# An adaLN attention and MLP block on one core: GpSimd's memsets after the first norm, modulation weights in halves of rows, one row tile's statistics on ScalarE, and the MLP transposes on TensorE

## The chip, the cores and the metric

The kernel runs on one core of a Trainium2 chip. The metric is the device time of one execution in microseconds; the time of a kernel is the median of several runs. The engines are TensorE (PE; its weight loads are listed as PEld), VectorE (DVE), ScalarE (ACT), GpSimd (POOL) and SyncE (SP), which issues nearly all DMAs here.

## The reference, cut to what matters

2048 tokens of width 512, 32 heads of 16, an MLP of width 1376, bf16 in and out.

```python
def _A_ref(x, wqkv, wo):                       # H = 32 heads, Dh = 16
    q, k, v = split((x @ wqkv))                # 2048 x 512 each
    p = softmax(einsum('bhqd,bhkd->bhqk', q, k) * Dh ** (-0.5))
    return merge(einsum('bhqk,bhkd->bhqd', p, v)) @ wo

def _B_ref(x, w1, b1, w2, b2):
    return gelu(x @ w1 + b1) @ w2 + b2         # tanh form of gelu

mod = (silu(c) @ w_mod).reshape(1, 6, 1, 512)  # w_mod is 512 x 3072
sa, ca, ga, sb, cb, gb = mod[:, 0], ..., mod[:, 5]
h = layernorm(x) * (1 + ca) + sa
x = x + ga * _A_ref(h, A_wqkv, A_wo)
h = layernorm(x) * (1 + cb) + sb
x = x + gb * _B_ref(h, B_w1, B_b1, B_w2, B_b2)
```

The softmax is over all 2048 keys for each head and query, so 32 x 2048 x 2048 exponentials are needed. Attention does not depend on the order of the tokens as long as queries, keys, values and outputs use the same one.

## The kernel before

**Tiling.** The tokens are four blocks of 512 (`QB`), each of four row tiles of 128 (`TPB`). The widths are handled in four chunks of 128 columns. Attention is cut into 32 runs: for blocks 0 to 2 a run is one block of queries and four heads, for the last block it is half a block of queries and eight heads. Each run goes over 16 key tiles of 128 keys; a key tile of a run is four pieces of 128x512 scores. TensorE makes scores (line 850), an engine makes exponentials, and TensorE multiplies them with the values (line 1042) into one accumulator `od`, where a column of ones in the values (`VEB`) makes the denominators.

**Two ways of making exponentials.** ScalarE takes two or three pieces at a time from the score tiles `st` with its Exp function (line 900, written to `pt`). VectorE takes pieces from the small PSUM tiles `ax` (line 948): it adds a constant to scaled scores and writes int16, whose bits are a bf16 of about the exponential; four shifted copies (lines 980 and 1001, a part of the last on GpSimd, line 986) are multiplied with the values as well, which evens out the error. Which key tiles VectorE may take is fixed per run (`DKS`, four of 16; one in the first run); ScalarE takes over those that VectorE has not begun when its own are used up.

**What sets the order.** The order of instructions on each engine is made when the kernel is built. `Plan` is a small model of the engines: every piece of work is an `Op` with an engine, an estimated duration, dependencies, a priority, sometimes a resource to acquire and a gate (a function that says whether it may be chosen yet). `Plan.step` picks the next one, and its instructions are written out at that moment. Dependencies of an `Op` set only when the planner lets it start; what waits on the chip follows from the tiles that instructions write and read, and from dependencies added by hand (`behind`, `after_dve`). Priorities get a pseudo-random part from the list `SEEDS`, one number for each 12.5 us of planned time. When TensorE would be idle, the planner adds matmuls on zeros (`heat`, lines 443, 448, 459).

**The front.** `c` goes through silu and one small transpose into `sc` (line 580, ScalarE). SyncE loads the first block of tokens in two halves (line 506), then two blocks of 512 columns of `w_mod` (`load_mod`, line 513), then the first columns of the projection weights (line 526), which are held by hand until the first of the two `w_mod` loads has landed (`behind`). `mod_half` (line 604) multiplies `sc` with one `w_mod` block into four columns each, the shift (line 609) and one plus the scale (line 611), into `modA`.

`layer_norm` (line 647) does the norm of one block: statistics of each row tile on VectorE (`stats`, lines 619 and 620), the reciprocal roots for two row tiles at a time on GpSimd (`rstd`, lines 624 and 626), the normalised rows `z` on VectorE (`apply`, line 630), the transpose, and the modulation (`modulate`, line 635 on ScalarE, line 638 on VectorE). For the norms ahead of attention, TensorE transposes `z` into PSUM (lines 669 and 690). For the MLP's, which have no pair of PSUM resources (the last branch), a DMA transposes each row tile from `z` into `h` (line 706), and the modulation works in place on `h` (line 712). `z`, `h`, `st`, `ax` and `modA` carry the names under which they appear in the profile; `h` is there as `blk`. Two `ax` tiles serve VectorE's scores and all projections.

GpSimd zeroes the query tiles `qm` (line 751) and sets up the value tiles `VEB` (line 561); for all but the first block a gate (`first_ln`) lets the planner choose these only after the first norm's `z` are placed.

**The tail of a block.** `block_tail` (line 1239) runs the output projection, the residual, the second norm and the MLP of a finished block between the attention work of later ones; the first half of the last block has the same function with two row tiles, the second half is `last_half` (line 1315).

Of the kernel before, what the change touches and what calls it, by code (L numbers as in the profile page):

```python
# [56 lines left out]
SEEDS = (0, 21, 549, 0, 302, 149, 169, 905, 398, 171, 86, 267, 11, 0, 921, 757, 414, 415, 365, 131, 15, 618, 871, 673, 0, 7, 415, 859, 670, 71, 663, 730, 487, 227, 515, 667, 435, 149, 398, 986, 54, 601, 378, 422, 797, 441, 478, 923, 570, 539, 723, 939, 122, 117, 263, 722, 826, 101, 751, 0, 366, 0, 0, 0, 0, 0)  # L57
# [196 lines left out]
def kernel(  # L254
# [211 lines left out]
    x_src = A_x[0].rearrange("(b t p) d -> b p t d", t=TPB, p=P)  # L466
# [136 lines left out]

    def mod_half(i):
        w = o_wm[i]
        mm = chain([(lambda ps, m=m: mod_mm(ps, 0, w.tile, m, False), 0.22, 0.17 * (m % 2) + 0.01)
                    for m in range(NC)], [o_sc, o_warm, w], "modA", r_ax, [w])
        if i == 0:
            return op("DVE", lambda o: nc.vector.tensor_copy(out=modA[:, 0:NC], in_=mm.tile[:, 0:NC]), 0.2, (mm,),
                      prio=0.0, rel=(mm,))  # L610
        return op("DVE", lambda o: nc.vector.tensor_scalar(out=modA[:, NC:2 * NC], in0=mm.tile[:, 0:NC], scalar1=1.0,
                                                           scalar2=None, op0=ALU.add), 0.2, (mm,), prio=0.0, rel=(mm,))
    o_mA = op("NIL", None, 0.0, [mod_half(i) for i in range(2)], lat=0.0, prio=0.0)


    def stats(ln, t, src):
# [3 lines left out]
        nc.vector.bn_aggr(out=mv[:, t, :], in_=st6)  # L620

# [25 lines left out]
    def layer_norm(src, deps, mod, mod_dep, hold_z, alloc_h, engines, ps_res, kind, prio,  # L647
                   after=None, nt=TPB, by_part=False):
# [908 lines left out]
```

## Time and profile before

| What | Value |
| --- | --- |
| runs | 778.5, 780.29, 780.5 us; median 780.29 |
| profiled execution, its time | 777.76 us |
| its span, first to last instruction | 776.0 us |
| granted TensorE clock, mean over the span | 0.997 |
| ScalarE busy outside the exponentials | 749.1 - 707.3 = 41.8 us |
| first exponential starts | 16.20 us |
| last group of exponentials ends | 751.7 us |
| DMA engines' mean busy share, 0 to 20 us | 0.71 |

Times are microseconds, unless a column is said to be nanoseconds. A line of a group gives the source line, engine, operation, output and input tiles, shapes, the count, then the busy time and the mean duration in nanoseconds of one, then how long the engine stood idle ahead of these instructions and what ended most of that. A line of a timeline gives start and duration, then the same names, and in brackets the idle time before it and what released it. A line of the windows gives the stretch, its length, the busy time of PE, PEld, DVE, ACT and POOL, the granted clock, the DMA share and GB/s.

### The profile page before, as it was taken

The page shows a single profiled execution, that of the slowest core. Times are in us where ns is not written, and L with a number is a line of the kernel's source. Part 1 is how long each engine was busy: PE and PEld are TensorE (multiplying, and loading weights), DVE is VectorE, ACT ScalarE, POOL GpSimd, SP SyncE. Part 2 cuts the span into 40 slices and gives each one's busy share as a digit, 9 for nine tenths or more (in the row PEclk, how much of TensorE's full clock was granted, in tenths as well). Part 3 has the DMA queues.
Part 4 walks back from the last instruction along what each step waited for, and adds up shares of the span by engine and source line. Part 5 has one row for each costly group of instructions (what it writes and reads, how often), then busy time and mean ns, then how long its engine had stood idle before and what let it go on. Part 6 is the DMA issues. An engine that isn't in the chain of part 4 may idle for free. (4 is left out here: it accounts for less than half of the span.)

```text
span 776.0 us, 20631 instructions
## 1 busy us (share of the span) xinstructions
PE 720.0 (93%) x8218; PEld 271.0 (35%) x8288; DVE 717.8 (93%) x1196; ACT 749.1 (97%) x683; POOL 279.3 (36%) x615
## 2 busy tenths in 40 slices
PE   8899989999999899999989999999999999999997
PEld 3433423323333222323222233323234344344444
DVE  6868899899999999999999999999989998999974
ACT  3999999999999999999999999999999999999993
POOL 6222433444443334344444333332232332233330
PEclk9999999999999999999999999999999999999999
DMA  7007011000011101110101200001111021000200
GB/s 217 29 17 215 18 25 43 20 17 16 19 45 27 47 20 50 32 21 22 44 20 35 44 18 24 19 21 32 33 44 31 26 40 46 17 19 25 64 20 28
DMA packets 46690, 30.07 MB, mean 39 GB/s; under 512 B 25573, under 2 KB 41990, under 8 KB 46594
## 3 DMA queue, kind: packets, MB, share of 16 engines
q1 hardware_dynamic: 46586, 28.75, 13.6%
q8 instruction: 65, 1.06, 0.6%
q14 instruction: 31, 0.25, 0.1%
q10 hardware_dynamic: 8, 0.00, 0.0%
HBM read 21.30 MB, written 2.61 MB: 31 GB/s over the span
## 5 line engine op out<-in xcount | busy, mean ns | idle before, releaser
L900 ACT ACTIVATE pt<-st 128x1536 bf16<-128x1536 f32 x624 | 707.3, 1419 | 2.2 <-PE ax L850 1.2
L948 DVE TENSOR_SCALAR ph<-ax 128x512 int16<-128x512 f32 x488 | 320.3, 682 | 22.3 <-PE ax L850 20.1
L986 POOL TENSOR_TENSOR sl<-ph,step 128x128 int32<-128x128 int32 x352 | 162.3, 463 | 316.2 <-DVE ph L1001 85.2
L850 PE MATMUL st<-qm,kT 32*128 32x512 bf16 x1560 | 243.8, 382 | 32.6 <-ACT pt L900 25.4
L850 PEld LDWEIGHTS <-kT 32*128 32x128 bf16 x2048 | 85.7, 91 | 244.0 <-issue 234.5
L850 PE MATMUL ax<-qm,kT 32*128 32x512 bf16 x488 | 159.8, 379 | 5.5 <-DVE ph L948 2.7
L1042 PEld LDWEIGHTS <-VEB 128*32 128x32 bf16 x5024 | 110.5, 95 | 154.0 <-issue 129.2
L1001 DVE TENSOR_SCALAR sh<-ph 128x4096 int16<-128x4096 int16 x122 | 148.3, 1217 | 0.1
L1042 PE MATMUL od<-pt,VEB 128*32 128x512 bf16 (+1 forms) x1944 | 148.1, 342 | 0.2 <-DVE OD L1067 0.2
L1042 PE MATMUL od<-ph,VEB 128*32 128x512 bf16 (+1 forms) x1232 | 90.8, 338 | 2.0 <-DVE ph L1001 0.7
L1042 PE MATMUL od<-sh,VEB 128*32 128x512 bf16 (+1 forms) x1232 | 87.8, 338 | 0.3
L1001 DVE TENSOR_SCALAR ph<-ph 128x2048 int16<-128x2048 int16 x122 | 83.3, 685 | 0.4
L980 DVE TENSOR_SCALAR sl<-ph 128x1024 int16<-128x1024 int16 (+3 forms) x122 | 59.2, 488 | 0.3
L1094 POOL TENSOR_TENSOR OT<-OD,RB 128x128 bf16<-128x128 f32 x76 | 34.5, 458 | 55.8 <-DVE sh L1001 28.3
L1042 PE MATMUL od<-sl,VEB 128*32 128x512 bf16 (+1 forms) x616 | 49.1, 338 | 0.4 <-POOL sl L986 0.2
L1265 PE MATMUL ax<-blk,W 128*128 128x512 bf16 (+1 forms) x156 | 41.1, 352 | 1.3 <-issue 0.5
L1094 POOL TENSOR_TENSOR OS<-OD,RB 128x128 bf16<-128x128 f32 x48 | 22.9, 479 | 41.2 <-DVE sh L1001 24.1
L729 PE MATMUL ax<-blk,w 128*128 128x512 bf16 x96 | 31.0, 386 | 1.0 <-issue 0.5
L1269 DVE TENSOR_SCALAR g<-ax,b1c 128x512 bf16<-128x512 f32 x33 | 24.4, 743 | 1.2 <-PE ax L1265 1.1
L1209 PE MATMUL ax<-w,g 128*128 128x512 bf16 x85 | 24.8, 382 | 0.7 <-DVE ph L948 0.3
L619 DVE BATCH_NORM_STATS2 ln_s<-xb 128x6 f32<-128x512 bf16 x32 | 21.7, 677 | 2.6 <-DMA xb<-in_A_x_dram 2.5
L1067 DVE COPY OD<-od 128x512 f32<-128x512 f32 x31 | 21.1, 682 | 0.0
(121 smaller groups left out, 398.7 us busy)
## 6 DMA issues: line engine op xcount, KB each, us to landing
RB<-rn SPq DMA_DIRECT2D x124, 64.0 KB
xb<-in_A_x_dram SPq DMA_DIRECT2D x8, 512.0 KB
out_dram<-o SPq DMA_DIRECT2D x16, 128.0 KB
qm<-qs SPq DMA_DIRECT2D x120, 16.0 KB
W<-in_B_w_dram SPq DMA_DIRECT2D x1, 1376.0 KB
w<-in_A_wqkv_dram SPq DMA_DIRECT2D x3, 384.0 KB
blk<-in_w_mod_dram SPq DMA_DIRECT2D x2, 512.0 KB
g<-in_w_mod_dram SPq DMA_DIRECT2D x2, 512.0 KB
```

The lines of the kernel that those rows point to most:

```text
L729: return chain([(lambda ps, j=j, n=n: nc.tensor.matmul(out=ps[:, 0:QB], lhsT=w.tile[:, j, cc * P:(cc + 1) * P], rhs=o_h[b].tile[:, j, :], ...
L850: nc.tensor.matmul(out=o.tile[:, k * QB:(k + 1) * QB], lhsT=kT[cc][kb][rows, ko * P:(ko + 1) * P], rhs=qm.tile[rows, par, :] if hb is None ...
L900: nc.scalar.activation(out=e.tile[:, 0:len(got) * QB], in_=o.tile[:, 0:len(got) * QB], func=ACT.Exp, scale=ESC)
L948: nc.vector.tensor_scalar(out=ph.tile[:, c0:c0 + QB], in0=o.tile, scalar1=PH_B, scalar2=0.0, op0=ALU.add, op1=ALU.max)
L980: parts = [in_turn(op("DVE", lambda o: nc.vector.tensor_scalar(out=into.tile[:, 0:cols], in0=first.tile[:, 0:cols], scalar1=PH_SH[-1], sca ...
L986: after_dve(nc.gpsimd.tensor_tensor(out=into.tile[:, c].bitcast(I32), in0=first.tile[:, c].bitcast(I32), in1=step, op=ALU.add))
L1001: o = op("DVE", lambda o: nc.vector.tensor_scalar(out=dst(o), in0=src(), scalar1=PH_SH[j], scalar2=None, op0=ALU.add), us, deps, lat=DL, p ...
L1042: nc.tensor.matmul(out=o_od[r].tile[32 * i:32 * i + 32, n * HB:n * HB + w], lhsT=v_tile(kt)[:, c0:c0 + 32], rhs=got[i][:, at:at + w], star ...
L1094: two = beside(lambda c: nc.gpsimd.tensor_tensor(out=OT.tile[:, c], in0=OD.tile[:, c], in1=o5.tile[:, c], op=ALU.mult), (OT,), (OD, o5))
L1209: nc.tensor.matmul(out=ps, lhsT=g[:, f, col:col + P], rhs=rhs, start=(f == 0), stop=(f == NF - 1))
L1265: mm = chain([(lambda ps, f=f, j=j: nc.tensor.matmul(out=ps[:, 0:N], lhsT=W1[:, j, f * P:(f + 1) * P], rhs=h.tile[:, j, 0:N], start=(j == ...
L1269: ev.append(op("DVE", lambda o, f=f, mm=mm: nc.vector.tensor_scalar(out=g.tile[:, f, 0:N], in0=mm.tile[:, 0:N], scalar1=b1c[:, f:f + 1], s ...
```

## The change

Five things change, and the planner's seeds with them.

- The planner's memsets of `qm` and `VEB` (all but the first block's) depend on the first norm's last `z`, where they had a gate.
- The two first loads of `w_mod` take 256 rows and 1024 columns each, where they took 512 rows and 512 columns; the products of the first half of the rows go to `modP`, and the second half's are added to them.
- Row tile t of a block holds tokens 4p + t on partition p, where it held tokens 128t + p; outputs are stored accordingly.
- The statistics of the first block's fourth row tile are made by ScalarE, in two passes with a running sum.
- The MLP's norms are transposed by TensorE into `ax`, from where the modulation reads them; there were DMA transposes, with the modulation in place in SBUF.

```diff
-SEEDS = (0, 21, 549, 0, 302, 149, 169, 905, 398, 171, 86, ...)
+SEEDS = (629, 934, 166, 131, 246, 833, 618, 433, 157, 123, ...)
...
-    x_src = A_x[0].rearrange("(b t p) d -> b p t d", t=TPB, p=P)
+    x_src = A_x[0].rearrange("(b p t) d -> b p t d", t=TPB, p=P)
+    out_dst = out[0].rearrange("(b p t) d -> b p t d", t=TPB, p=P)
...
     def load_mod(i):
         def go(o):
-            first[i] = nc.sync.dma_start(out=o.tile, in_=wm_src[:, :, i * D:(i + 1) * D])
+            first[i] = nc.sync.dma_start(out=o.tile.rearrange("p (j h) n -> p j (h n)", h=2),
+                                         in_=wm_src[:, 2 * i:2 * i + 2, 0:2 * D])
...
-    def v_init(v, prio, gate):
+    def v_init(v, prio, after):
         x = v[..., 0:32 * VW].rearrange("p t (h w) -> p t h w", w=VW)
-        return [op("POOL", lambda o, to=to, c=c: nc.gpsimd.memset(to, c), 0.35, prio=prio, gate=gate)
+        return [op("POOL", lambda o, to=to, c=c: nc.gpsimd.memset(to, c), 0.35, after, prio=prio)
...
-    first_ln = [False]
-    for b in range(NQ):
-        late = (lambda: True) if b == 0 else (lambda: first_ln[0])
-        o_v0[b] = v_init(VEB[b], 1.0 + b, late)
+    o_v0[0] = v_init(VEB[0], 1.0, ())
...
     def mod_half(i):
         w = o_wm[i]
-        mm = chain([(lambda ps, m=m: mod_mm(ps, 0, w.tile, m, False), 0.22, 0.17 * (m % 2) + 0.01)
-                    for m in range(NC)], [o_sc, o_warm, w], "modA", r_ax, [w])
+        def go(ps, m):
+            for j in range(2):
+                nc.tensor.matmul(out=ps[:, m:m + 1], lhsT=w.tile.rearrange("p (j h) n -> p j (h n)", h=2)[
+                    :, j, m * P:(m + 1) * P], rhs=sc[:, 2 * i + j:2 * i + j + 1], start=(j == 0), stop=(j == 1))
+        mm = chain([(lambda ps, m=m: go(ps, m), 0.08, 0.17 * (m % 2) / 2 + 0.005) for m in range(2 * NC)],
+                   [o_sc, o_warm, w], "modA", r_ax, [w])
         if i == 0:
-            return op("DVE", lambda o: nc.vector.tensor_copy(out=modA[:, 0:NC], in_=mm.tile[:, 0:NC]), 0.2, (mm,),
-                      prio=0.0, rel=(mm,))
-        return op("DVE", lambda o: nc.vector.tensor_scalar(out=modA[:, NC:2 * NC], in0=mm.tile[:, 0:NC], scalar1=1.0,
-                                                           scalar2=None, op0=ALU.add), 0.2, (mm,), prio=0.0, rel=(mm,))
+            one = op("DVE", lambda o: nc.vector.tensor_copy(out=modP[:, 0:NC], in_=mm.tile[:, 0:NC]), 0.12, (mm,),
+                     prio=0.0, rel=(mm,))
+            two = op("DVE", lambda o: nc.vector.tensor_scalar(out=modP[:, NC:2 * NC], in0=mm.tile[:, NC:2 * NC], scalar1=1.0,
+                                                              scalar2=None, op0=ALU.add), 0.12, (mm,), prio=0.0, rel=(mm,))
+            return op("NIL", None, 0.0, (one, two), lat=0.0, prio=0.0)
+        return op("DVE", lambda o: nc.vector.tensor_tensor(out=modA, in0=mm.tile[:, 0:2 * NC], in1=modP, op=ALU.add),
+                  0.2, (mm, parts[0]), prio=0.0, rel=(mm,))
...
+    def stats_act(ln, t, src):
+        mv, _ = ln.tile
+        root = math.sqrt(D)
+        junk = work.tile([P, D], BF16, name="ln_j", bufs=1)
+        neg = work.tile([P, 1], FP32, name="ln_n", bufs=1)
+        nc.scalar.activation(out=junk, in_=src, func=ACT.Identity, scale=-1.0 / (D * root), accum_out=neg)
+        nc.scalar.activation(out=junk, in_=src, func=ACT.Square, bias=neg, scale=1.0 / root,
+                             accum_out=mv[:, t, 1:2])
+        nc.scalar.mul(mv[:, t, 0:1], neg, -root)
...
-        st = [op("DVE", lambda o, t=t: stats(ln, t, src(t)), 0.83, (deps[t], ln, after and after[t]), prio=prio)
+        st = [op("ACT", lambda o, t=t: stats_act(ln, t, src(t)), 1.7, (deps[t], ln), prio=prio) if t in on_act else
+              op("DVE", lambda o, t=t: stats(ln, t, src(t)), 0.83, (deps[t], ln, after and after[t]), prio=prio)
...
-            turned = [dma(lambda o, t=t: nc.sync.dma_start(
-                out=h.tile[:, :, t * P:(t + 1) * P], in_=z.tile[:, t, :], transpose=True),
-                (za[t], h), kb=P, n=2.8, prio=0.6, rel=(z,)) for t in range(nt)]
             for j in range(NC):
+                def tr(o, j=j):
+                    o.ps = o.tile.bitcast(BF16)[:, 0:nt * P]
+                    for t in range(nt):
+                        nc.tensor.transpose(out=o.ps[:, t * P:(t + 1) * P],
+                                            in_=z.tile[:, t, j * P:(j + 1) * P], identity=ident)
+                one = op("PE", tr, nt * 0.0705, za, lat=PEL, mode=("full", 0), kind=kind,
+                         acq=r_ax, rel=(z,))
+                trs.append(one)
                 e = engines[j]
-                done.append(op(e, lambda o, j=j, e=e: modulate(
-                    e, h.tile[:, j, 0:nt * P], h.tile[:, j, 0:nt * P], mod, j), 0.07 + nt * 0.068, turned + [mod_dep, h],
-                    prio=0.1, port=True))
+                done.append(op(e, lambda o, j=j, one=one, e=e: modulate(
+                    e, h.tile[:, j, 0:nt * P], one.ps, mod, j), 0.13 + nt * 0.1, (one, mod_dep, h), prio=0.1,
+                    rel=(one,)))
...
-    o_qz = [op("POOL", lambda o, n=n, p=p: nc.gpsimd.memset(QM[n][:, p, :], 0.0), 0.5, prio=0.5 + n, gate=lambda: first_ln[0])
-            for n in range(1, 4) for p in range(2)]
+    o_qz = []
...
-                out=out[0][b * QB + t * P:b * QB + (t + 1) * P, :], in_=a.tile), (a,), kb=128,
+                out=out_dst[b][:, t, :], in_=a.tile), (a,), kb=128,
...
-            ("DVE", "ACT") if b in PARTS else ("DVE", "DVE", "ACT", "ACT") if b < 3 else ("DVE",) * 4, tuple(r_st[::-1]) if b == 0 else (r_ax, r_ax), kind, 0.6 + 0.2 * b, after, by_part=b in PARTS)
+            ("DVE", "ACT") if b in PARTS else ("DVE", "DVE", "ACT", "ACT") if b < 3 else ("DVE",) * 4, tuple(r_st[::-1]) if b == 0 else (r_ax, r_ax), kind, 0.6 + 0.2 * b, after, by_part=b in PARTS,
+            on_act=() if b else (3,))
...
         if b == 0:
-            op("NIL", lambda o: first_ln.__setitem__(0, True), 0.0, za, lat=0.0, prio=0.0)
+            o_qz.extend(op("POOL", lambda o, n=n, p=p: nc.gpsimd.memset(QM[n][:, p, :], 0.0), 0.5, za[-1:], prio=0.5 + n)
+                        for n in range(1, 4) for p in range(2))
+            for nv in range(1, NQ):
+                o_v0[nv] = v_init(VEB[nv], 1.0 + nv, za[-1:])
```

More of the change, by code (lines that the diff above doesn't have):

```diff
@@ L602, in mod_columns @@
         return op("DVE", out_, 0.4, (mm,), prio=0.65, rel=(mm,))
+    modP = const.tile([P, 2 * NC], FP32, name="modP")
     def mod_half(i):
         w = o_wm[i]
[L606 to L613 removed]
+        def go(ps, m):
[4 more added lines that the diff above has]
+                   [o_sc, o_warm, w], "modA", r_ax, [w])
+        if i == 0:
+            one = op("DVE", lambda o: nc.vector.tensor_copy(out=modP[:, 0:NC], in_=mm.tile[:, 0:NC]), 0.12, (mm,),
[5 more added lines that the diff above has]
+                  0.2, (mm, parts[0]), prio=0.0, rel=(mm,))
+    parts = []
+    for i in range(2):
+        parts.append(mod_half(i))
+    o_mA = parts[1]
     def stats(ln, t, src):
@@ L1412, in last_half @@
             dma(lambda o, t=t, a=a: nc.sync.dma_start(
-                out=out[0][b * QB + t * P:b * QB + (t + 1) * P, :], in_=a.tile), (a,), kb=128,
+                out=out_dst[b][:, t, :], in_=a.tile), (a,), kb=128,
                 rel=(a,))
```

4 lines of the change are left out of this document (2 added, 2 removed).

## The prediction

> **What bounds the kernel now.** I read the page first (engine shares, costliest groups), then busy time by windows, then the timeline of the first 17 us, then single shapes. From the page:
>
> ```profile
> span 776.0 us, 20631 instructions
> PE 720.0 (93%) x8218; PEld 271.0 (35%) x8288; DVE 717.8 (93%) x1196; ACT 749.1 (97%) x683; POOL 279.3 (36%) x615
> ...
> L900 ACT ACTIVATE pt<-st 128x1536 bf16<-128x1536 f32 x624 | 707.3, 1419 | 2.2 <-PE ax L850 1.2
> L948 DVE TENSOR_SCALAR ph<-ax 128x512 int16<-128x512 f32 x488 | 320.3, 682 | 22.3 <-PE ax L850 20.1
> ...
> L1001 DVE TENSOR_SCALAR sh<-ph 128x4096 int16<-128x4096 int16 x122 | 148.3, 1217 | 0.1
> ...
> L1001 DVE TENSOR_SCALAR ph<-ph 128x2048 int16<-128x2048 int16 x122 | 83.3, 685 | 0.4
> L980 DVE TENSOR_SCALAR sl<-ph 128x1024 int16<-128x1024 int16 (+3 forms) x122 | 59.2, 488 | 0.3
> ```
>
> ScalarE's exponentials (L900) take 707 us and wait 2.2 us in all. A key tile is four 128x512 pieces of one run; there are 32 runs of 16 tiles, 512 in all. VectorE took 122 of them (L948 has 488 = 4 x 122), ScalarE the other 390. A tile costs ScalarE 4 x 707.3/1560 = 1.81 us, and VectorE (320.3 + 148.3 + 83.3 + 59.2)/122 = 5.01 us. Busy time by windows of 100 us (PE, PEld, DVE, ACT, POOL, clock, DMA):
>
> ```profile
> 200.00:300.00 100.00, 94.16 (x1018) 32.49 (x1021) 98.13 (x154) 100.00 (x90) 39.11 (x87) 1.00 0.13 34
> 600.00:700.00 100.00, 94.98 (x1473) 41.62 (x1481) 95.45 (x159) 99.94 (x86) 33.49 (x73) 1.00 0.12 31
> ```
>
> ScalarE has no gap in the long middle and VectorE almost none. So the time is three terms: the front until the first exponential (16.2 us), ScalarE's unbroken work (to 751.7 us), and a tail of 24.3 us. The middle gets shorter only if tiles move to VectorE. If VectorE gets x us more of other work, the two share it: x/5.01 / (1/1.81 + 1/5.01) = 0.27x us on the end. The front, from its timeline (start, duration, engine):
>
> ```profile
> 6.76 0.70 DVE L630 TENSOR_SCALAR z<-xb,mv,rs 128x512 bf16<-128x512 bf16 x2
> 6.93 0.29 POOL L624 TENSOR_SCALAR rs<-mv 128x2 f32<-128x2 f32 x1 [0.56 <-DVE mv L620]
> 7.30 0.74 POOL L626 TENSOR_TENSOR rs<-rs,mhalf 128x2 f32<-128x2 f32 x1
> 7.99 0.99 POOL L751 MEMSET qm<- 128x512 bf16 x2
> 8.36 0.16 DVE L609 COPY modA<-ax 128x4 f32<-128x4 f32 x1 [0.90 <-PE ax L586]
> 8.44 2.12 DVE L630 TENSOR_SCALAR z<-xb,mv,rs 128x512 bf16<-128x512 bf16 x2
> 10.62 0.93 PE L690 MATMUL st<-ident,z 128*128 128x128 bf16 x7 [0.78 <-DVE modA L611]
> 11.16 0.99 DVE L638 TENSOR_SCALAR blk<-st,modA 128x512 bf16<-128x512 bf16 x2 [0.53 <-PE st L690]
> 12.21 0.62 PE L729 MATMUL st<-blk,w 128*128 128x512 bf16 x1 [0.23 <-DVE blk L638]
> 16.20 6.88 ACT L900 ACTIVATE pt<-st 128x1536 bf16<-128x1536 f32 x6 [0.64 <-PE st L850]
> ```
>
> Statistics, rs, the four z, transposes, modulation, projections, scores, exponential: one chain. The second pair of z takes 2.12 us beside GpSimd's memsets, the first pair 0.70 without them. The clock (the last three columns are granted clock, DMA share, GB/s):
>
> ```profile
> 10.00:11.00 1.00, 0.38 (x4) 0.39 (x5) 0.63 (x2) 0.00 (x0) 1.00 (x3) 0.74 0.82 172
> 12.00:13.00 1.00, 0.79 (x2) 0.29 (x2) 0.15 (x1) 1.00 (x2) 1.00 (x4) 0.50 1.11 350
> 14.00:15.00 1.00, 1.00 (x10) 0.53 (x9) 0.58 (x3) 0.03 (x1) 0.00 (x0) 1.00 0.96 300
> ```
>
> From about 10.3 to 13.7 us TensorE ran at half clock, just where transposes and projections stand.
>
> **The change, part by part.**
>
> *Statistics of the fourth row tile on ScalarE.* VectorE loses one BATCH_NORM pair (0.66 + 0.18 us, 0.80 from start to start) and finishes the third at 6.05 instead of the fourth at 6.84. ScalarE does two passes of 128x512; the nearest row is its modulation, 1.45 us for two, plus 0.17 for a small ACTIVATE: 1.6 us, and what the running sum costs is not in the trace: between nothing and two more small ones (0.34). I take 1.8. The row tile is there between 4 and 5.17 us (VectorE took its neighbour at 5.17 without a wait); taking 4.5, ScalarE ends at 6.3, idle there anyway (3.59 us idle before L580). GpSimd's rs, at 6.93 before, starts at about 6.5 and ends at 7.6, not 8.04. `sc` (6.51) stands behind these passes on ScalarE; if they ended at 7, it and the modulation matmuls would be late by 0.5 us; these have that cover only while the weights land at 7.74.
>
> *Modulation weights in halves of rows, tokens by partition.* Bytes are the same; rows get 2 KB instead of 1 KB. The two modulation loads flow from about 4 to 9.1 us, 1 MB in 5.1 us, against 300 to 350 GB/s in the windows at 12 to 15 us, which would be 3.0 to 3.5. So between 0 and 2 us can go; I take 0.4 for the first load (7.74 to 7.3), nearer to nothing, since the engines were already busy with it most of the time (DMA share 0.91 and 0.90 in 5 to 7 us). One more small VectorE copy, 0.15. The column matmuls stay at 32. Projection weights wait for the first load and move with it. Out stores keep 1 KB rows, scattered by 4 KB: 0, off the path but for the last store.
>
> *The second pair of z.* It starts at 8.44 because L609 stands ahead of it in VectorE's queue and waits for the weights. If that order stays: 8.2. If the earlier rs puts z first: 7.6. I take z first, -0.84, since rs is now planned earlier than the weights; the other end is -0.2.
>
> *Memsets depend on the first norm.* The dependency is one of the planner's: it sets when a memset is planned, and issues no semaphore (where the code wants a real one it adds it by hand, as in `after_dve`). On GpSimd nothing stands between the second rs and the memsets before or after. I take 0; the bounds are 0 and -1.4 (2.12 - 0.70). In a sentence by itself: the Trainium skill's page "SBUF — State Buffer", section on the shared port pair, says that a VectorE operation of the two-port kind and a GpSimd one exclude each other; the 2.12 us agree, and if the change really kept the memsets out, the sum would be 1.4 us lower.
>
> *Clock.* Four of the eight projection matmuls start 0.42 us apart, not 0.21 (0.8 us), and the seven transposes took 0.93 where eight took 0.61 at full clock (0.4): 1.2 us. Before the drop TensorE stood idle 0.78 us for z; with z 0.84 earlier this gap goes. I take the whole 1.2; the ends are 0 and, if the drop moves onto the projections entirely, +0.8. The Trainium skill ("TensorE: Matmul & The Clock Gate", Part 1) says the window is free-running, about 3.4 us; the trace's stretch is that long, and by this rule the phase differs from run to run, so half the gain, 0.6, would be the mean, and the sum below 0.6 higher.
>
> *Front: -0.84 - 1.2 = -2.0 us* (from -3.4, with the memsets, to +1.0).
>
> *MLP transposes on TensorE.* 14 DMA transposes go (4 in each of three blocks, 2 in the last), with 1.2 us each of SyncE's queue and the 28 us that the queue stood at L706. TensorE on the critical side waited 1.0 us in all for the q rows of that queue: gain 0 to 1.0, taken 0. Added: 16 transposes a block and 8 in the last, 56; eight take 0.62, so 4.3 us of TensorE, hidden behind its fillers (L443 and L459: 20 us of records that are planned only where TensorE is free); without that cover it would be late for scores and cost 4.3. The modulation now reads PSUM:
>
> ```profile
> L638 DVE TENSOR_SCALAR blk<-blk,modB 128x512 bf16<-128x512 bf16 x12 | 4.3, 402 | 0.0
> L638 DVE TENSOR_SCALAR blk<-blk,modB 128x256 bf16<-128x256 bf16 x4 | 1.1, 344 | 0.0
> L638 DVE TENSOR_SCALAR blk<-ax,modA 128x256 bf16<-128x256 bf16 x8 | 2.7, 406 | 0.1
> L638 DVE TENSOR_SCALAR blk<-ax,modA 128x512 bf16<-128x512 bf16 x4 | 2.0, 540 | 1.3 <-PE ax L690 1.3
> ```
>
> 12 x 0.138 + 4 x 0.062 = 1.9 us of VectorE, so 0.27 x 1.9 = +0.5. Each of the 16 also takes one of two `ax` tiles from VectorE's scores: between nothing and one mean wait of L948 (20.1/38 = 0.53 us); I take nothing here.
>
> *New seeds.* The order is drawn anew. VectorE can take at most 125 tiles (4 a run, 1 in the first), 3 more, each 1.33 us by the shared rate and 1.81 at most: -5.4 at best, as much the other way for three fewer; the tail's order can shift by some 1.5. Taken 0.
>
> *Sum:* -2.0 + 0.5 = -1.5. The profiled execution took 777.76 us (span 776.0 and 1.76 around it), so 776.3; the median of the runs is 780.29, 2.5 above it, so **778.8**.
>
> **The rivals.**
>
> *VectorE becomes the bound (slower).* Place: the two `ax` tiles in the MLP blocks. If each of the 16 new takings costs L948 its 0.53 us, 8.5 + 1.9 = 10.4 us of VectorE, two whole tiles go back to ScalarE: 3.6 us; with 1.2 saved in the front and one tile more lost to the new order (1.3), 780.3 + 3.6 - 1.2 + 1.3 = 784. It decides from 2.3/0.27 = 8.5 us of VectorE upwards if the front gives nothing. For it: VectorE is 95 to 99% busy and PE ax is its main wait. Against: `ax` is already taken for some 50 q, k and v projections, and L1269 (33 evictions from `ax`) waited 1.2 us in all.
>
> *More goes to VectorE (faster).* SyncE's queue is free of 45 us of issue and standing, the front is about -2.9, and two of the three tiles move: 780.3 - 2.9 + 0.5 - 2.7 = 775. For it: VectorE still idles 20 us between 100 and 740 us. Against: those gaps are waits for TensorE, which gets more to do.
>
> *It doesn't do what it says.* Memsets run beside z as before, weights land as before, z stays behind the copy; the front gives 0 to 0.5, and +0.5 in the middle cancels it: 780.3.
>
> **How the numbers follow.** What a measurement of this kernel can tell is about 0.3%, 2.3 us. Forecast 0.48, its own range 776.5 to 781 (front -3.4 to 0, middle 0 to +1), of which 0.2 lies below 778.0. VectorE gains 0.18. VectorE bound 0.27. Nothing happens 0.07. Faster 0.2 + 0.18 = 0.38, and 0.02 more from the forecast with a better tail: 0.40; slower 0.27 and 0.02 from a worse tail: 0.29; the rest, 0.31, within. The range reaches from 773 (two tiles and the whole front) to 785 (the slower rival and a tail 1 us worse).
>
> **What would show it.** First L900 at about 14.2 us; rs for the third and fourth tiles at 6.5; z pair still about 2.1 us long beside L751; granted clock 1.00 in 10 to 14 us; L948 about 488 +- 4; L638 from `ax` at 0.54 us; L948's wait for PE ax near 20 us. It is wrong if L948 drops below 480, if ScalarE shows gaps in the middle, or if the first exponential isn't earlier.

## The result, and the profile after

The changed kernel takes 780.97 us (median of 20 runs, 778.18 to 785.15), the kernel before 778.40 us (20 runs, 776.91 to 781.29). The ratio is 1.0032, with a 95% interval of 1.0016 to 1.0048: it became slower by 2.5 us. The median of three runs that the prediction started from, 780.29, was 1.9 us above that of 20. Of all the runs of the experiments, one (821.81 us, the profiled run of the query rows one after the other) was in a slower state of the chip, and medians and ratios leave it out.

From here on, line numbers are those of the kernel that a line comes from; L927 of the changed kernel is L900 of the one before, L975 is L948, and L877 is L850. First the page of the changed kernel, to be laid beside the first lines of the prediction:

```profile
span 779.1 us, 20699 instructions
PE 732.7 (94%) x8299; PEld 276.2 (35%) x8299; DVE 713.5 (92%) x1188; ACT 752.8 (97%) x690; POOL 283.2 (36%) x632
...
L927 ACT ACTIVATE pt<-st 128x1536 bf16<-128x1536 f32 x626 | 708.9, 1408 | 5.1 <-PE st L877 3.2
L975 DVE TENSOR_SCALAR ph<-ax 128x512 int16<-128x512 f32 x484 | 317.6, 683 | 27.1 <-PE ax L877 24.6
```

L975 has 484 pieces, not 488: VectorE got 121 tiles, one fewer, and it waits longer for TensorE (24.6 us against 20.1) though it has less to do. ScalarE's exponentials now wait 5.1 us, not 2.2. Windows of the changed kernel (PE, PEld, DVE, ACT, POOL, clock, DMA share, GB/s):

```profile
500.00:600.00 100.00, 96.16 (x1095) 33.79 (x1097) 95.16 (x149) 98.36 (x84) 30.92 (x68) 0.98 0.10 28
600.00:700.00 100.00, 94.14 (x1470) 42.05 (x1462) 94.33 (x157) 98.02 (x84) 34.34 (x77) 1.00 0.10 28
```

In the last one ScalarE was busy 99.94 us before and is busy 98.02 now. Its timeline (start, length of an unbroken group, and in brackets the wait ahead of it) shows where; first the changed kernel, then the kernel before:

```profile
563.03 11.47 ACT L927 ACTIVATE pt<-st 128x1536 bf16<-128x1536 f32 x10 [1.33 <-PE ax L877]
...
606.15 78.32 ACT L927 ACTIVATE pt<-st 128x1536 bf16<-128x1536 f32 x69 [1.92 <-PE st L877]
...
755.93 1.28 ACT L1301 ACT_TABLE_LOAD   x1
```

```profile
573.38 5.99 ACT L900 ACTIVATE pt<-st 128x1536 bf16<-128x1536 f32 x5 [0.25 <-PE st L850]
580.31 88.25 ACT L900 ACTIVATE pt<-st 128x1024 bf16<-128x1024 f32 x78 [0.94 <-PE ax L850]
...
751.70 1.28 ACT L1274 ACT_TABLE_LOAD   x1
```

The table load ends the exponentials: 755.93 against 751.70. With the first exponential at 15.97 against 16.20 us, the two profiled executions differ like this:

| Term | Before | After | Difference |
| --- | --- | --- | --- |
| front, to the first exponential | 16.20 | 15.97 | -0.23 |
| middle, to the last table load | 735.50 | 739.96 | +4.46 |
| tail, to the end of the span | 24.30 | 23.17 | -1.13 |
| span | 776.0 | 779.1 | +3.1 |

Of the 4.46, one tile more on ScalarE is 1.81. The listed waits of its exponentials between 20 and 752 us sum to 3.67 (0.17, 1.33, 0.25, 1.92) against 1.47 (0.28, 0.25, 0.94), which is 2.20 more. By the windows from the first exponential to the last table load, ScalarE was busy 735.85 us against 733.73, 2.12 more, and idle 2.34 more: the tile is most of the first, the listed waits are most of the second.

The granted clock explains part of the spread of the runs: among those with a mean clock of 0.999 or more, the changed kernel's median is 778.65 (5 of 20 runs), that of the kernel before 777.51 (13 of 31 runs beside the first experiments), which leaves 1.1 of the 2.5 us. The mean over all of these runs is 0.9966 for the changed kernel and 0.9976 for the kernel before.

The front of the changed kernel:

```profile
5.66 1.06 PE L443 MATMUL ax<-warm 128*128 128x512 bf16 x2
...
7.89 0.17 PE L576 MATMUL ax<-ident,sr 4*128 4x4 bf16 x1
...
9.62 0.54 PE L610 MATMUL ax<-sc,blk 128*128 128x1 bf16 x16 [0.15 <-PE ax L443]
```

```profile
6.26 0.74 DVE L652 TENSOR_SCALAR z<-xb,mv,rs 128x512 bf16<-128x512 bf16 x2 [0.36 <-POOL rs L648]
10.20 0.16 DVE L617 TENSOR_SCALAR modP<-ax 128x4 f32<-128x4 f32 x1 [3.20 <-PE ax L610]
10.27 0.15 DVE L615 COPY modP<-ax 128x4 f32<-128x4 f32 x1
10.34 0.85 DVE L652 TENSOR_SCALAR z<-xb,mv,rs 128x512 bf16<-128x512 bf16 x2
```

```profile
8.10 0.17 ACT L579 ACTIVATE sc<-ax 128x4 bf16<-128x4 bf16 x1 [2.04 <-PE ax L576]
```

The first modulation matmul (L610) needs its weights and `sc`, which ScalarE had at 8.27 us. SyncE has one wait for these weights, 4.2 us long; it issues two loads of projection columns ahead of it (2.64 and 3.15 us) and the next at 8.05, when the wait is over. So the weights landed at about 8.05 us, not earlier than in the kernel before (7.74), and L610 stood ready from 8.27 to 9.62 us, 1.35 us, behind fillers (L443, L448) on TensorE's queue. In the kernel before, its counterpart was released by the weights:

```profile
7.77 0.46 PEld L586 LDWEIGHTS <-blk 128*128 128x128 bf16 x16 [0.60 <-DMA blk<-in_w_mod_dram]
```

The second pair of z stood behind the two copies of the columns on VectorE, which waited 3.20 us for L610.

This front is one draw. Five of the experiments below leave its instructions as they are (without the MLP transposes, more fillers, one tile fewer, and both on the query rows), and their profiles have the first exponential at 15.22, 15.69, 15.08, 16.03 and 15.88 us. In all six, L610 starts 1.72 or 1.73 us behind the small transpose of L576, with the same fillers between the two. What moves is L576, from 6.87 to 7.89 us: the fillers ahead of it start 0.43 us apart at first and 0.22 apart later, and the step from one to the other lies anywhere between 4.8 and 6.9 us. The clock column reads 1.00 on both sides of it, so this step is read from the spacing alone.

### The profile page after: what moved, and what is told of

The parts are those of the page before. It is cut to its first block, busy times and chain, and to the rows that moved or that the text cites. A ratio compares the mean times of both kernels' runs of the same rounds, so it can differ in the third digit from the quotient of the medians.

```text
span 779.1 us, 20699 instructions
## 1 busy us (share of the span) xinstructions
PE 732.7 (94%) x8299; PEld 276.2 (35%) x8299; DVE 713.5 (92%) x1188; ACT 752.8 (97%) x690; POOL 283.2 (36%) x632
## 4 chain that ended last, share of the span: by engine, by line
ACT 52%; PE 31%; issue 9%; DVE 7%; SPq 1%; DMA 0%; POOL 0%; DVEq 0%; ACTq 0%; POOLq 0%
ACT pt L927 50%; PE od L1069 10%; PE st L877 9%; DVE ph L975 3%; PE ax L1292 2%; PE ax L1236 2%; PE ax L877 2%; PE ax L757 2%; PE t L1236 1%; DVE sh L1028 1%; PE ax L443 1%; PE ax L1230 1%; DVE ph L1028 1%; PE t L1421 1%; ACT g L1307 1%
## 5 line engine op out<-in xcount | busy, mean ns | idle before, releaser
L927 ACT ACTIVATE pt<-st 128x1536 bf16<-128x1536 f32 x626 | 708.9, 1408 | 5.1 <-PE st L877 3.2
L975 DVE TENSOR_SCALAR ph<-ax 128x512 int16<-128x512 f32 x484 | 317.6, 683 | 27.1 <-PE ax L877 24.6
L1013 POOL TENSOR_TENSOR sl<-ph,step 128x128 int32<-128x128 int32 x369 | 168.9, 459 | 315.3 <-DVE sh L1028 103.0
L877 PE MATMUL st<-qm,kT 32*128 32x512 bf16 x1564 | 245.0, 382 | 29.1 <-ACT pt L927 22.3
L877 PEld LDWEIGHTS <-kT 32*128 32x128 bf16 x2048 | 88.2, 91 | 247.3 <-issue 233.6
L877 PE MATMUL ax<-qm,kT 32*128 32x512 bf16 x484 | 160.5, 380 | 5.3 <-DVE ph L975 2.7
L1069 PE MATMUL od<-pt,VEB 128*32 128x512 bf16 (+1 forms) x1952 | 144.7, 342 | 0.1
L1069 PE MATMUL od<-sh,VEB 128*32 128x512 bf16 (+1 forms) x1216 | 85.3, 339 | 0.9 <-DVE sh L1028 0.9
L1121 POOL TENSOR_TENSOR OT<-OD,RB 128x128 bf16<-128x128 f32 x76 | 34.3, 455 | 69.7 <-DVE sh L1028 20.1
L1007 DVE TENSOR_SCALAR sl<-ph 128x1024 int16<-128x1024 int16 (+4 forms) x121 | 58.4, 484 | 0.4 <-PE od L1069 0.2
L1069 PE MATMUL od<-sl,VEB 128*32 128x512 bf16 (+1 forms) x608 | 47.5, 340 | 0.3 <-DVE VEB L667 0.3
L1292 PE MATMUL ax<-blk,W 128*128 128x512 bf16 (+1 forms) x176 | 44.0, 355 | 0.5 <-DVE ph L975 0.2
L757 PE MATMUL ax<-blk,w 128*128 128x512 bf16 x116 | 34.3, 391 | 0.1
```

Of the source, the lines that this page charges most:

```text
L757: return chain([(lambda ps, j=j, n=n: nc.tensor.matmul(out=ps[:, 0:QB], lhsT=w.tile[:, j, cc * P:(cc + 1) * P], rhs=o_h[b].tile[:, j, :], ...
L877: nc.tensor.matmul(out=o.tile[:, k * QB:(k + 1) * QB], lhsT=kT[cc][kb][rows, ko * P:(ko + 1) * P], rhs=qm.tile[rows, par, :] if hb is None ...
L927: nc.scalar.activation(out=e.tile[:, 0:len(got) * QB], in_=o.tile[:, 0:len(got) * QB], func=ACT.Exp, scale=ESC)
L975: nc.vector.tensor_scalar(out=ph.tile[:, c0:c0 + QB], in0=o.tile, scalar1=PH_B, scalar2=0.0, op0=ALU.add, op1=ALU.max)
L1007: parts = [in_turn(op("DVE", lambda o: nc.vector.tensor_scalar(out=into.tile[:, 0:cols], in0=first.tile[:, 0:cols], scalar1=PH_SH[-1], sca ...
L1013: after_dve(nc.gpsimd.tensor_tensor(out=into.tile[:, c].bitcast(I32), in0=first.tile[:, c].bitcast(I32), in1=step, op=ALU.add))
```

## The experiments

All ratios are to the kernel before, run beside the experiment on the same chip. The changed kernel stands at 1.0032.

### One part of the change undone, the order kept

The first runs keep every engine's order as the planner made it for the changed kernel; only what an instruction does is changed.

**Without the MLP transposes.**

```diff
-                    o.ps = o.tile.bitcast(BF16)[:, 0:nt * P]
-                    for t in range(nt):
-                        nc.tensor.transpose(...)
+                    o.ps = z.tile[:, 0:nt, j * P:(j + 1) * P]
```

> The changed kernel in its own order of instructions, without the 56 transposes of the MLP norms (left out: the turning; the modulation reads the normalised rows from SBUF, so the output is not the reference's). Theory 'TensorE transposes': 4.3 us of TensorE and 1.9 us of VectorE go, the half-clock stretch at 556 to 559 us may go with them, and the time falls by 1.5 to 3 us against the changed kernel. Theory 'order': the order fixes 121 tiles on VectorE and where scores wait, so the time falls by less than 0.7 us.

Measured: 780.50 us, ratio 1.0023 (1.0009 to 1.0037), 0.5 us under the changed kernel's median, 0.7 by the ratios, and within the intervals of both. Its profile has the same wait near 604 us (2.10), none listed near 563, and VectorE waits as long for TensorE as with the transposes:

```profile
L972 DVE TENSOR_SCALAR ph<-ax 128x512 int16<-128x512 f32 x484 | 317.4, 683 | 28.4 <-PE ax L874 26.0
```

From its first exponential to the table load it takes 739.50 us, against 739.96 in the changed kernel and 735.50 before. The order theory's side, if not by much: the transposes as executed are not where most of the 2.5 us went.

**DMA rows as before.**

```diff
-            first[i] = nc.sync.dma_start(out=... "p j (h n)" ..., in_=wm_src[:, 2 * i:2 * i + 2, 0:2 * D])
+            for h in range(2):
+                first[i] = nc.sync.dma_start(out=... "p j h n" ...[:, :, h, :],
+                                             in_=wm_src[:, 2 * i:2 * i + 2, h * D:(h + 1) * D])
```

and `(b t p)` for both token layouts.

> The changed kernel in its own order, with the rows of the DMAs as before: tokens 128t + p on partition p, and each modulation load issued as two DMAs with rows of 1 KB. If the larger rows are worth something at the front, the first exponential comes 0.5 to 1 us later and so does the end. If TensorE's queue of fillers holds the front (its first modulation matmul stood at 9.62 us, with its weights there at 6.9), nothing moves: under 0.3 us.

Measured: 781.03 us, 1.0032 (1.0010 to 1.0053). Nothing moved at the end. The first exponential came at 15.13 us, not later, but fronts without any edit differ by as much (15.08 to 16.03). SyncE's wait for the first weights ended at 7.41 us, against 8.05 in the changed kernel and 7.25 to 8.10 in its other profiles with the larger rows: the 6.9 us of the expectation was misread. So no gain of the larger rows shows in this order.

**The fourth row tile's statistics on VectorE.** `stats_act(ln, t, src(t))` becomes `stats(ln, t, src(t))`, at the same place.

> The changed kernel in its own order, with the fourth row tile's statistics on VectorE again, at the same place of the order. If ScalarE's statistics are worth something, rs comes 0.4 us later and the end 0.4 us later. If TensorE's queue of fillers holds the front, nothing moves: under 0.3 us, since the second pair of z waited for the modulation columns until 10.3 us.

Measured: 782.20 us, 1.0041 (1.0021 to 1.0061). The second rs starts at 6.81 us instead of 6.21, as expected, and the pair of z again waits for the columns. The median is 1.2 us higher, but the intervals overlap: inconclusive for the end, and the mean clock of these runs was lower as well (0.9952).

**Thinner fillers in the front.** The filler matmuls ahead of the first scores take 256 columns.

```diff
-                out=o.tile, lhsT=warm, rhs=warm[:, 0:1].to_broadcast([P, QB]), ...
+                out=o.tile[:, 0:fill_n()], lhsT=warm, rhs=warm[:, 0:1].to_broadcast([P, fill_n()]), ...
```

> The changed kernel in its own order, with the fillers of the front 256 columns wide in place of 512 (what they compute is thrown away). Theory 'fillers hold the front': the first modulation matmul moves from 9.6 to about 7.5 us, the first exponential from 16.0 to about 14.5, and the median falls by 1 to 2 us. Rival 'clock': the thinner fillers leave TensorE at half clock, the projections take 1.2 us more, and the time stays or rises by up to 1 us.

Measured: 782.73 us, 1.0041 (1.0018 to 1.0064). TensorE in its profile:

```profile
7.41 0.55 PE L613 MATMUL ax<-sc,blk 128*128 128x1 bf16 x16 [1.31 <-DMA blk<-in_w_mod_dram]
...
11.87 0.63 PE L760 MATMUL st<-blk,w 128*128 128x512 bf16 x1
12.30 0.63 PE L760 MATMUL ax<-blk,w 128*128 128x512 bf16 x1
```

Both theories were right about their half. The first modulation matmul moves from 9.62 to 7.41 us and is now released by its weights, which SyncE saw at 7.38: the fillers did hold the front. But the projections run at half clock (0.63 us, granted clock 0.50 from 9 to 15 us), and the first exponential comes at 16.34 us, later than before.

### What the middle answers to

**More fillers at two weak places.** One more group of matmuls on zeros behind each value product while the planner's time is 546 to 551 or 594.5 to 597.5.

> The changed kernel in its own order, with one more matmul group on zeros behind each value product at two weak places, about 552 to 557 and 601 to 604 us, where TensorE waits and after which the clock was halved in several profiles. Theory 'clock': such stretches get rarer there, the spread of the runs narrows, and the median falls by 0.5 to 1.5 us. Rival: the added matmuls stand in front of scores and the time rises by up to 1 us.

Measured: 781.19 us, 1.0037 (1.0022 to 1.0052). The mean granted clock of its 12 runs rose to 0.9993 (0.9966 for the changed kernel) and their spread fell to 779.87 to 783.86, but the median did not fall. At an equal mean clock (0.999 or more) it is 781.14, 2.5 us above the changed kernel's 778.65, as the rival has it. ScalarE still waits 1.18 us at 563 and 1.47 at 605 us. The clock can be held, but at this price nothing is won.

**One tile fewer on ScalarE.** Two exponentials of 128x1024 are replaced by GpSimd memsets.

> The changed kernel in its own order, with four pieces of exponentials near the middle (one key tile's worth) left out on ScalarE and set to zero by GpSimd, so that the output is not the reference's. If ScalarE is what bounds the middle, the time falls by one tile, 1.8 us, against the changed kernel, which is what one tile more on VectorE would give. If TensorE or VectorE bounds it, less than 0.6 us.

Measured: 781.64 us, 1.0045 (1.0027 to 1.0062). A miss, for a reason its timeline shows: three new waits of ScalarE near 360 to 373 us (0.55, 0.55, 0.69), close to the two memsets (359.1 and 369.9 us), took back 1.79. ScalarE was ahead of the changed kernel's profile by 0.89 us at the first exponential and by 0.61 at 434.92 (435.53 there), so nothing of the tile was left by then; at 563 the rest was gone, behind a wait of 2.08 in place of 1.33. So it doesn't tell a tile's price.

**Query rows one after the other**, for all query tiles, then for the one that is late at 604 us.

```diff
+                def move(o, at, p):
+                    if not moved and 583.0 < plan.now < 594.0:      # all tiles in the first try
+                        moved.extend(...)
+                        for x, y in moved:
+                            nc.sync.dma_start(out=qm.tile[x:x + 16, y, :], in_=qs.tile[x:x + 16, :])
```

> The changed kernel in its own order, except that the eight small DMAs of each query tile are issued one right after the other, where other transfers stood between them on SyncE's queue. Theory 'order': the wait for query rows near 604 us (1.9 us of ScalarE, in each of the profiles so far) shrinks below 1 us, and the time falls by 0.7 to 1.5 us against the changed kernel. Theory 'TensorE transposes': nothing, under 0.4 us.

Measured: 812.52 us, 1.0431 (1.0392 to 1.0471). In its profile ScalarE waits 24.1 us for scores, and the wait that was near 604 us is still there (2.42, now at 646). The edit puts eight DMAs ahead of other small transfers on SyncE's queue for every query tile, which presumably delays those; it says nothing about the one wait.

> The changed kernel in its own order, except that the eight row DMAs of one query tile (last block, third chunk, issued at 597 to 604 us) go one right after the other on SyncE's queue, ahead of two small transfers that stood between them. If that wait (1.9 us of ScalarE in the changed kernel's profile) makes the middle longer by itself, it falls below 1 us and the time by 0.5 to 1.5 us against the changed kernel. If it only takes up what was gained before, another wait behind it grows and the time stays within 0.4 us.

Measured: 782.13 us, 1.0050 (1.0033 to 1.0067). SyncE's queue and, below it, ScalarE:

```profile
597.46 6.01 SPq L799 DMA_DIRECT2D qm<-qs  x8
603.51 0.58 SPq L1108 DMA_DIRECT2D dc<-dn  x1
```

```profile
606.17 1.45 ACT L933 ACTIVATE pt<-st 128x1536 bf16<-128x1536 f32 x1 [2.05 <-PE st L883]
```

The eight take 6.0 us to issue by themselves, and the wait is as long as it was (2.05 us). The transfers between them were not the reason. VectorE writes this query tile at 596.5 us, which is too late for eight such DMAs, and that is set by where the order puts its projection.

### The order without its random part

With all seeds 0 the planner takes the first choice by priority alone. Four kernels: before and after, each with either way of transposing. Each still has an order of its own, since the edits change what is planned.

```diff
-SEEDS = (...)
+SEEDS = (0, 0, 0, ...)
```

> The kernel before with all seeds 0, so that the order has no random part. VectorE gets 115 tiles, 7 fewer than with the seeds drawn for it. Theory 'order': 7 tiles are 9 to 13 us on the end, so the time rises to 787 to 793 us; if the drawn order is worth little, under 782.

> The changed kernel with all seeds 0; 116 tiles on VectorE. Theory 'order': without the drawn seeds the edits are no loss, so it is not slower than the kernel before with all seeds 0, and 0 to 4 us faster (one tile more, and the front). Theory 'the edits cost': it is 1 to 3 us slower than that, as the changed kernel is.

> The kernel before with the MLP transposes on TensorE alone, all seeds 0; 116 tiles on VectorE; same order as the kernel before with all seeds 0 until the first block's MLP. Theory 'TensorE transposes cost': 1.5 to 3 us slower than the kernel before with all seeds 0. Theory 'order': within 2 us of it, on either side, by the tile and the waits that the order happens to give.

> The changed kernel with the MLP transposes by DMA again, all seeds 0; 115 tiles on VectorE; against the kernel before with all seeds 0 only the front differs at first. If the front edits are worth something, 0.5 to 1.5 us faster than the kernel before with all seeds 0 and the first exponential earlier by as much; if later waits take it back, the same within 0.5.

| All seeds 0 | Tiles on VectorE | Median us | Ratio (95%) |
| --- | --- | --- | --- |
| before | 115 | 805.83 | 1.0342 (1.0298 to 1.0386) |
| before, TensorE transposes | 116 | 805.14 | 1.0338 (1.0303 to 1.0374) |
| after, DMA transposes | 115 | 800.77 | 1.0274 (1.0240 to 1.0307) |
| after | 116 | 802.79 | 1.0320 (1.0265 to 1.0376) |

Before and after, all seeds 0, the exponentials and VectorE's pieces:

```profile
L900 ACT ACTIVATE pt<-st 128x1536 bf16<-128x1536 f32 x635 | 722.1, 1354 | 9.9 <-PE od L1042 5.6 <-PE st L850 1.7 <-PE ax L850 1.7
L948 DVE TENSOR_SCALAR ph<-ax 128x512 int16<-128x512 f32 x460 | 303.0, 685 | 42.2 <-PE ax L850 40.1 <-POOL sl L986 0.6
```

```profile
L927 ACT ACTIVATE pt<-st 128x1536 bf16<-128x1536 f32 x634 | 720.6, 1370 | 15.8 <-PE st L877 6.6 <-PE od L1069 5.3 <-PE ax L877 3.5
L975 DVE TENSOR_SCALAR ph<-ax 128x512 int16<-128x512 f32 x464 | 306.7, 686 | 52.8 <-PE ax L877 49.9 <-POOL sl L1013 1.1
```

In the kernel before the seeds are worth 28 us (805.83 against 777.88 beside it), in the changed kernel about 22 (802.79 against 1.0032 times 777.88). Without them VectorE stands idle 42 and 53 us, mostly for scores, and gets 7 and 5 tiles fewer; the mean clock is lower too, 0.984 to 0.990 against 0.998. I expected 787 to 793 us from the tiles alone; the waits and the clock come on top. Next to this the edits are small, and four runs of each, which spread over 5 to 9 us, don't resolve them. TensorE transposes alone change nothing in the kernel before (1.0338 against 1.0342); in the changed kernel they stand 2.0 us above the DMA transposes, with overlapping intervals. The changed kernel is not shown to be slower than the kernel before here. The lowest median, 1.0274 for the front edits with DMA transposes, is not a shorter front: its profile has the first exponential at 16.77 us, where the kernel before with all seeds 0 has it at 15.45.

### The front alone, in either order

**Real waits of the memsets, in the kernel before.**

```diff
+    def late_set(to, c, wait=True):
+        got = nc.gpsimd.memset(to, c)
+        if wait:
+            tc.add_manual_dep(got.ins, z_last[0].ins.name, ..., reason="after z")
```

> The kernel before in its own order, with a real wait: GpSimd's memsets of the query tiles and of the later value tiles wait for the first norm's last z. If the memsets are what made the second pair of z 2.12 us long, the pair takes 0.7 us, the modulation starts up to 1.4 us earlier, and the end comes 0.5 to 1.4 us earlier. If it was something else, the pair stays near 2.1 us. The rival for the end: GpSimd's memsets now run into the next block's rs and the gain is given back.

Measured: 777.23 us, 0.9985 (0.9970 to 1.0000). VectorE, then GpSimd:

```profile
8.87 0.73 DVE L637 TENSOR_SCALAR z<-xb,mv,rs 128x512 bf16<-128x512 bf16 x2
...
14.03 0.69 DVE L626 BATCH_NORM_STATS2 ln_s<-xb 128x6 f32<-128x512 bf16 x1 [2.55 <-DMA xb<-in_A_x_dram]
```

```profile
9.66 0.99 POOL L568 MEMSET qm<- 128x512 bf16 x2 [1.64 <-DVE z L637]
```

The pair takes 0.73 us, not 2.12: the memsets were what stretched it. The modulation starts at 10.49 instead of 11.16, yet the first exponential comes at 16.07, so the 0.9 us between the medians is not the front's, and the interval reaches 1. What is late next is in the second line: VectorE stands 2.55 us at the second block's statistics, waiting for that block's load, with the query evictions queued behind.

**That statistics instruction put behind the query evictions as well**, then also tokens 4p + t on a partition.

```diff
+        n_st[0] += 1
+        if n_st[0] == TPB + 1:
+            put_off.append((ln, t, src))
+            return
...
+                if p:
+                    stats(*put_off.pop())
```

> The kernel before in its own order, with GpSimd's memsets really waiting for the last z, and the second block's first statistics put behind the two query evictions on VectorE instead of in front of them, where they waited 2.55 us for the block's load. First exponential at about 14.8 us instead of 16.1. If the end follows the front, 1.2 to 2.0 us faster than the kernel before; if the middle takes it back, under 0.9.

> As g1, with tokens 4p + t on partition p as well, so that the loads of blocks of tokens have rows of 4 KB. If the larger rows land sooner, the second block's first statistics need not wait and the time is 0 to 0.5 us under that of g1; if the load is bound by what is queued ahead of it, the same.

Measured: 777.01 us, 0.9983 (0.9967 to 0.9999), and 776.38 us, 0.9971 (0.9962 to 0.9981). The first exponential of each, the first run above:

```profile
14.89 3.71 ACT L917 ACTIVATE pt<-st 128x1536 bf16<-128x1536 f32 x3 [0.64 <-PE st L867]
```

```profile
13.90 4.62 ACT L918 ACTIVATE pt<-st 128x1536 bf16<-128x1536 f32 x4 [0.64 <-PE st L868]
```

In the order of the kernel before, the end follows the front: 1.31 us earlier at the first exponential and 1.0 at the end of the span (775.0), then 2.30 and 1.8 (774.2). The second is faster than the kernel before, by 2.3 us at the medians of its comparison (776.38 and 778.70). Part of this is the clock: the profile of the kernel before has TensorE at half clock from 10.3 to 13.7 us, these two have not, and among runs with a mean clock of 0.999 or more the medians are 777.51, 776.56 and 776.38, so 1.0 and 1.1 us remain. The profiles are of one execution each; in the second the copy of the modulation columns starts 0.6 us earlier (8.36 against 8.99), and how much of that is due to its layout of tokens is not separated.

**Real waits of the memsets, in the changed kernel.**

> The changed kernel in its own order, with GpSimd's memsets really waiting for the first norm's last z. The second pair of z takes 0.7 us, the modulation comes 0.2 to 0.9 us earlier. If the end follows the front, 0.2 to 0.9 us faster than the changed kernel; theory 'order': the waits near 563 and 604 us take it back and the time stays within 0.4 us.

Measured: 781.82 us, 1.0027 (1.0005 to 1.0048); the changed kernel is at 1.0032.

```profile
14.37 4.63 ACT L935 ACTIVATE pt<-st 128x1536 bf16<-128x1536 f32 x4 [1.30 <-PE st L885]
```

```profile
562.09 11.47 ACT L935 ACTIVATE pt<-st 128x1536 bf16<-128x1536 f32 x10 [1.99 <-PE ax L885]
...
605.27 1.45 ACT L935 ACTIVATE pt<-st 128x1536 bf16<-128x1536 f32 x1 [1.97 <-PE st L885]
607.64 77.12 ACT L935 ACTIVATE pt<-st 128x1024 bf16<-128x1024 f32 x68 [0.91 <-PE ax L885]
```

The pair takes 0.73 us, and the first exponential is 1.60 us earlier than in the changed kernel's profile. The real wait didn't do that: the first modulation matmul already starts 1.61 us earlier (8.01 against 9.62), since the fillers came closer together sooner in this execution, and from there to the first exponential it is 6.36 us against 6.35. The pair that the changed kernel's profile has beside memsets took only 0.85 us. The lead is 0.94 at 563 us, and behind 607 us it is gone: near 563 and 604 us ScalarE waits for scores, and these waits eat what it is ahead.

## Why the prediction was wrong

It forecast 778.8 us, 1.5 below the time before; the kernel became 2.5 us slower. The step that failed is "New seeds. ... Taken 0": the order drawn anew was treated as a noise of whole tiles around nothing, and it is the largest term of all. Of the prediction's own signs of being wrong, ScalarE's gaps in the middle came true. That 780.97 still lies inside its own range (776.5 to 781) is luck: the time that it started from was 1.9 us too high.

- **The order (taken 0).** In the profile the middle grew by 4.46 us, of which the prediction had 0.5. One tile less on VectorE and 2.2 us of waits at two places account for 4.0. No edit undone by itself takes this back: from first exponential to table load the changed kernel takes 739.96 us, 739.50 without the transposes and 741.21 with the old rows, and 738.3 to 745.3 over nine profiles in this order, while four profiles in the order of the kernel before have 735.5 to 736.5. All seeds 0 shows the scale, 22 to 28 us for the draw. What was not run is the same edits under other seeds, so the draw isn't separated from what the edits do to the plan. The price of the one tile, 1.81 us, rests on counts and durations; the experiment on it missed.
- **The waits in the middle (not in the sum).** The wait near 604 us is in all nine profiles of this order (1.29 to 3.19 us). That near 563 us goes with the clock: it is 1.33 to 2.08 us in the four that have a stretch at half clock between 550 and 570 us, and 0.4 or less in four of the other five (the fifth, with more fillers, has 1.18). In the changed kernel's profile this stretch lies at 556 to 560 us, behind gaps of TensorE of 0.36 and 0.53 us at 554 and 555 us, while ScalarE ran the MLP's gelu. Why some executions have it and others not stays open.
- **The front (-2.0), mis-sized.** It measured -0.23, and by the draws of the same front -0.2 to -1.1. The statistics on ScalarE did come earlier: rs at 6.21 instead of 6.93. The weights did not: 8.05 instead of 7.74. "I take z first" was wrong: the copies of the columns stayed ahead of z on VectorE. And what the columns wait for was missed altogether, TensorE's queue of fillers, 1.73 us of them between L576 and L610. The bound given for this part (+1.0) did hold, though the ends listed for z and clock (-0.2 and +0.8) add up to +0.6.
- **The clock (-1.2).** It was at 1.00 from 10 to 14 us, as forecast; but in this execution the fillers were 0.43 us apart, twice their later spacing, up to 6.9 us, which delayed the columns. The Trainium skill's page "TensorE: Matmul & The Clock Gate" (Part 1) says the window is free-running, which would let the same front end at different times from execution to execution. The profiles agree: with the same instructions the fillers come closer from 4.8 us in one and only from 6.9 in another, and the first exponential lies between 15.08 and 16.03 us. The one profile of the kernel before, with half clock at its projections, may be such a draw as well.
- **Memsets (taken 0).** Right: the dependency is the planner's alone, and on GpSimd they begin right behind the second rs as before. That a real wait would bring the pair to 0.7 us was right too (0.73); the 1.4 us at the end were not, since other waits stood behind it. In the changed order the pair takes 0.85 to 1.72 us, by when it meets the memsets, and the way from L610 to the first exponential 6.35 to 7.11.
- **TensorE transposes (+0.5).** The instructions cost what was said: L660 from `ax` takes 529 and 404 ns where 402 and 344 were, 12 x 0.127 + 4 x 0.060 = 1.8 us of VectorE against 1.9. On the end, 0.5 us by leaving them out, and -0.7 and +2.0 with all seeds 0, all within the uncertainty. The rival of the two `ax` tiles had the sign right, VectorE's wait for TensorE grew by 4.5 us, but without the transposes that wait is still 26.0 us, and the time didn't come back.
- **The tail (taken 0)** is 1.1 us shorter. It goes with the order: 23.1 to 23.6 us in the profiles of this one, without the transposes too (23.2), and 24.3 in those of the order before.

## What to carry to other kernels

Where a search fits a static order to one program, an edit can't be costed apart from the search: compare both programs in the same order, keeping the order and changing what an instruction does, or in several orders, before a gain or a loss is put down to the edit. In a front, ask of each instruction that the path needs which instruction stands ahead of it in its own queue, fillers among them. A gain ahead of a long bound stage reaches the end only if no later wait in that stage is paced by another engine. And where executions of the same front differ by 1 us, compare distances inside it (from one instruction to the next that needs it), not the times at which it ends in one profile each.

## What the runs showed of the hardware

- GpSimd's memsets, mostly of 128x512 bf16, stretched a pair of VectorE operations of 128x512 bf16 in SBUF from 0.73 to 2.12 us; with VEB's narrow strided memsets beside most of it the pair took 0.85. The Trainium skill's page "SBUF — State Buffer" (Who interferes with whom) has the two engines exclude each other for whole instructions when VectorE's is in a two-port mode. The first figure agrees; the second is milder than that reading.
- Fillers are a price as well as a cover. At 512 columns they held the first modulation matmul until 9.62 us, 1.35 us after its operands were there; at 256 it came at 7.41, and TensorE then had half clock for the projections (0.50 from 9 to 15 us).
- Issuing eight 16 KB DMAs between SBUF tiles from one queue took 6.0 us, 0.75 us each, which is what a late query tile costs before its last rows are under way.
